# A fused attention and mixer kernel: batch 0's values loaded packed and unpacked by matmuls, a fourth block with a seven-product first layer, whole-half differences, and a new hand-written order

## Chip, cores and metric

One core of a Trainium2 chip runs the whole program. The metric is the device time of one execution in microseconds (us); the figure for a kernel is the median of its runs. The kernel before was measured three times: 341.62, 341.87 and 342.3 us.

## What is computed

The reference, cut to what matters (B=8 batches, H=8 heads, S=576 tokens, Nb=16 beacon rows, D=64):

```python
k_all = concat([beacon_k, k], axis=2); v_all = concat([beacon_v, v], axis=2)
a = softmax(causal(q @ k_all.T / sqrt(D)))          # beacon rows are never masked
x = (a @ v_all), heads side by side                 # 8 x 576 x 512
u = x + (xT @ U @ V).T                              # rank 32, mixes tokens
out = u + relu(u @ w_ch1) @ w_ch2                   # 512 -> 2048 -> 512
```

## The kernel before

**Attention** goes by pairs of heads: 32 pairs, four to a batch. For a pair the queries and keys are regrouped by token (`regroup`, L253), transposed either by PE (`qkT_units`, L261 to L268) or by a DMA transpose whose result is then put in token order by a copy from the tile `raw` (`order_units`, L291), and multiplied in four score visits (L316), each followed by two exponentials on ACT (L321). The causal mask is a minimum on DVE (L304, L306). `av_unit` (L331) multiplies with the values in 15 matmuls of 65 columns; the 65th column of the value tile holds ones, so the row sums come with it, and DVE divides (L339, L340). A batch's result goes through the rank-32 mixing (`mix_units`: qtp L371, ups L390 and L397) into the ring buffer `uT`.

**The mixer** takes `uT` in nine blocks of 512 tokens. Its second layer is always a Strassen-Winograd scheme with seven products P1 to P7 of half size (`product`, L620), for which DVE makes three operand sums per half (`operand_sum`, L601) and closes each product with an addition (`finish`, L645). Its first layer has two forms. Blocks 0 to 5 use sixteen plain units `g` (L529: four matmuls of 512 columns each); blocks 6 to 8 use 28 units `F` (`first_product`, L566: seven products, four pieces each, four matmuls of 256 columns a unit), with weight sums `wf` (L489) and token sums (`token_sum`, L508).

The second layer needs the quarter n3 minus the quarter a11. Before, each `g` unit of the lower half makes that difference on the way out of PSUM: ACT writes the first 256 columns (L533) and DVE the other 256 with a fused relu and subtraction (L534). In the seven-product blocks DVE does it with a fused operation in place (L583), the relu of product 2 is POOL's (L587) and that of product 7 ACT's (L589).

**Loads.** Batch 0's queries and keys come through the queues of SP and ACT (`load_first`); everything else is issued by POOL. `v_loads` (L203) writes values straight into the head-by-head tile `vs`, in five pieces and a beacon load per half or whole batch, so each packet it writes is one head's row of 64 half floats, 128 bytes.

**The order** is written by hand: a string SCRIPT of some 950 steps is walked once, and each step appends its instructions to the engines it uses, which run them in that order. The letters: `Sa` to `Sd` a pair's score visits, `M` the mask, `A` the value products of one head, `G` regroup, `T` transposition or ordering, `R` DMA transpose of a pair, `X` mixing, `g`, `F`, `p`, `P` the mixer's units, `V` a token sum, `U` a transpose of u, `k q v b w` loads, and `I1` one matmul that does no work but keeps PE running (L241). A letter A, V or G inside a step names the engine that copies: ACT, DVE or POOL.

Of the kernel before, what the change touches and what calls it, by code (L numbers as in the profile page):

```python
# [17 lines left out]
P = 128  # L18
# [9 lines left out]
def kernel(  # L28
# [101 lines left out]
    Vsb = const.tile([P, S], F16, name="Vsb", tag="Vsb")  # L130
    ones = const.tile([P, 1], F16, name="ones", tag="ones")
# [66 lines left out]
    def v_loads(src, bsrc, vs, hs):  # L198
        dst = vs[:, :].rearrange("p (c h e) -> p c h e", h=H, e=E)[:, :, hs, 0:D]
        beacon_load(nc.gpsimd, bsrc, dst[:, 0, :, :], hs)  # L200
        for j in range(NT):
            a = Nb if j == 0 else 0
            nc.gpsimd.dma_start(  # L203
                out=dst[a : a + nq[j], j, :, :], in_=src[hs, ds(q0[j], nq[j]), :].rearrange("h p d -> p h d")
            )

# [148 lines left out]
    def mix_units(xb, u0, xt=None, shifted=True):  # L355
# [24 lines left out]
        def part(a, e):  # L380
            n = e - a
            ups = [pst([P, n], F32, name="ups") for _ in range(NCC)]
# [108 lines left out]
    def token_sum(t, i):  # L491
# [16 lines left out]
        nc.vector.tensor_tensor(out=out, in0=a, in1=b, op=ALU.subtract)  # L508

    def block_steps(t, dst):  # L510
# [12 lines left out]
        def g_unit(dc):  # L523
# [8 lines left out]
            if dc < NK:  # L532
                nc.scalar.activation(out=gT[:, dc, 0:H2], in_=g[:, 0:H2], func=AF.Relu)  # L533
                nc.vector.scalar_tensor_tensor(  # L534
                    out=gT[:, dc, H2:512], in0=g[:, H2:512], scalar=0.0, in1=gT[:, dc, 0:H2],
                    op0=ALU.max, op1=ALU.subtract,
                )
            else:
                nc.scalar.activation(out=gT[:, dc, :], in_=g, func=AF.Relu)  # L539
# [4 lines left out]
        def first_product(n, mp):  # L544
# [18 lines left out]
            ps = banks[bank, mp]  # L563
            for i in range(2):
# [14 lines left out]
            else:  # L579
                out, other = {2: (a11, 1), 3: (n3, 6), 7: (a22, 5)}[n]  # L580
                nc.vector.tensor_tensor(out=out, in0=ps, in1=held[other, mp], op=ALU.add)  # L581
                if n == 3:
                    nc.vector.scalar_tensor_tensor(  # L583
                        out=n3, in0=n3, scalar=0.0, in1=a11, op0=ALU.max, op1=ALU.subtract
                    )
                elif n == 2:
                    nc.gpsimd.tensor_scalar_max(out=out, in0=out, scalar1=0.0)  # L587
                else:
                    nc.scalar.activation(out=out, in_=out, func=AF.Relu)  # L589

        def operand_sum(h, j):
# [7 lines left out]
            s2, s1, s4 = (sT[:, i, k, :] for i in range(3))  # L599
            out, x, y, op = ((s2, a22, n3, ALU.add), (s1, s2, a11, ALU.add), (s4, a12, s2, ALU.subtract))[j]  # L600
# [85 lines left out]

    COPY = {"V": nc.vector.tensor_copy, "G": nc.gpsimd.tensor_copy, "A": act_copy}
# [91 lines left out]
    def mix_of(b, part):  # L779
        if b not in mixes:  # L780
            head, parts = mix_units(xbs[b], S * b, xts.get(b))
            mixes[b] = [head] + parts
            for t in range(NBLK - NBR):
                assert 512 * (t + NBR) >= S * (b + 1) or uses[t] == NDC + NCC, (b, t)
# [4 lines left out]
    def step(t):  # L789
# [7 lines left out]
        elif name in "kqbv":  # L797
# [7 lines left out]
            else:  # L805
                v_loads(v[b], beacon_v[b], vss[b % 2], hs)
        elif name == "u":
            late["c"], late["e"], late["s"] = small_loads()
        elif name == "B":
            fill_bigmask()  # L810
        elif name == "s":
# [19 lines left out]
        elif name in "gpUPF":  # L831
# [22 lines left out]
        B I1 GqA0 HqA0 I1 I1 I1 k1A I1 b1 I1 HkV0 GkV0 TkV0 v0A TqA0 Sa0:3 I1 GqG1 u I1 GkV1 TkV1 GkA4  # L854
        I1 Sb0 I1 I1 I1 TqV1 Sd0 q1A Sc0 I1 M0.0 GkV3 I1 I1 Sa1:2 I1 GqV2 I1 Sb1 M0.1 I1 I1 GkG2 I1 TkA2
        TqV2 TkA4 I1 q1B I1 w10 v0B w12 GqA4 I1 Sc1 A0.0 TkV3 Sd1 GqV3 I1 A0.1 Sd2 Sb2 Sa2:1 I1 Sc2 M1.1
        s M1.0 TqV3 GkG5 I1 A1.1 A1.0 Sc3 GqV6 Sa3:1 M2.1 I1 cG I1 I1 GqV5 k1B Sb3 TqV6 I1 Sd3 TqA4 w13
        M2.0 eA k2 M3.1 M3.0 I1 TqA5 A2.1 A2.0 Sc4 Sa4 TkV5 I1 A3.1 GqA7 I1 I1 A3.0 Sd5 Sc5 GkV7 TqV7
        X0.0 Sd4 GkA6 I1 X0.2 X0.1 I1 U0.0 Sa5:0 v1A Sb4 Sb5 g0.8 TkA7 GkV9 M5.1 M4.1 GkV11 M4.0 g0.1
        M5.0 g0.15 g0.0 b2 TkA6 U0.1 GkV8 g0.10 q2 A5.1 A5.0 Sb7 Sa7 Sd7 w11 A4.1 A4.0 g0.11 GqV9 g0.3  # L860
        Sc7 GqV8 M7.1 M7.0 g0.12 Sb6 Sd6 TqV8 TkV9 TkV11 TqV9 g0.2 Sa6:0 GqA11 Sc6 M6.0 v1B g0.14 g0.5
        M6.1 g0.6 g0.9 A6.0 A7.1 A7.0 TkA8 A6.1 w20 g0.13 p00.0 w21 g0.4 Sc9 Sd8 X1.0 g0.7 p01.0 X1.2
        X1.1 p01.1 P01.0 GkV10 p00.1 W0 Sd9 U1.1 TqA11 Sb9 Sa8 W4 W5 W1 P02.0 W2 W3 U0.2 v2 W6 P01.1
        GqA10 Sc8 Sb8 U0.3 M8.1 p00.2 M8.0 P02.1 TkA10 P05.0 Sa9 b3 p01.2 TqA10 P05.1 P06.0 P06.1 A8.0
        b4 k3 GkA13 A8.1 Sa10 Sc10 M9.1 P03.0 P03.1 q3 q4 P07.0 A9.1 g1.9 g1.8 M9.0 A9.0 W7 Sb11 Sc11
        g1.2 g1.7 Sb10 Sd10 M10.0 GqV12 GkV12 R12 g1.1 g1.15 GqA14 Sa11 GqV13 R13 GkA14 R14 Sd11 M11.1
        g1.5 P07.1 g1.3 A10.0 g1.0 TkV12 M11.0 M10.1 g1.6 g1.12 TqA12 GqV16 A11.1 g1.10 TkV13 P04.0 U1.0
        U1.3 TqA13 GkA15 P04.1 g1.14 A11.0 k4 A10.1 Sa13 Sd12 g1.11 p10.0 g1.4 GqA17 g1.13 Sa12 Sb12
        Sc12 p11.0 GqV15 X2.0 M12.0 P11.0 GkA17 P11.1 U1.2 X2.1 GkV16 p11.1 R15 P12.0 P12.1 R16 P16.0
        TqV14 Sd13 Sb13 M12.1 p10.1 p10.2 Sc13 P16.1 b5 U2.2 M13.0 TkA14 v3 A12.1 q5 A12.0 R17 GkA19  # L870
        P15.0 P15.1 p11.2 Sa14 Sd14 Sc14 x12 P17.0 TkV15 M13.1 P13.0 U2.3 A13.0 Sb14 Z16 M14.0 P17.1
# [157 lines left out]
```

## Time and profile before

| what | value |
|---|---|
| median of the runs shown | 341.87 us |
| the profiled execution | 341.91 us |
| its span, first to last instruction | 340.3 us |
| PE, DVE, ACT, POOL busy | 330.1, 263.4, 228.3, 103.6 us |
| first unit of the mixer starts on PE | 36.91 us |
| last matmul starts | near 335 us |

The span is from the first to the last instruction; 1.6 us of the execution lie outside it. PE is the engine that runs the matmuls; its busy time is a union of overlapping spans, so a busy PE says only that some matmul was in flight, and the spacing of matmul starts is the better measure. In the tables a row gives busy time, the mean of one instruction and, after the second bar, how long the engine stood idle before it and for whom. In a timeline row the two first numbers are start and length.

### The profile page before, as it was taken

The numbers are of one execution on the slowest core, as the hardware profiler recorded it, in microseconds if no ns is written. First come the engines' busy times: TensorE is split into PE (matmuls) and PEld (weight loads), VectorE is DVE, ScalarE is ACT, GpSimd is POOL, SyncE is SP. The second block draws the span as 40 slices with busy tenths as digits, with TensorE's granted clock in tenths as the row PEclk, the third lists the DMA queues.
The fourth block names the chain that finished last, engine by engine and source line by source line (L and its number), as shares of the span: only waits on it lengthen the run. The fifth ranks groups of instructions, "written<-read, shape, count | busy, mean of one in ns | idle before, by whom it ended". The sixth has DMA issues, their size and how long they took to land.

```text
span 340.3 us, 8963 instructions
## 1 busy us (share of the span) xinstructions
PE 330.1 (97%) x3527; PEld 227.9 (67%) x3527; DVE 263.4 (77%) x681; ACT 228.3 (67%) x495; POOL 103.6 (30%) x137
## 2 busy tenths in 40 slices
PE   6989999999999999999999999999999999999994
PEld 2456555684668755775577646765688888888883
DVE  3489687994869766984888768885999999896872
ACT  3779987849787889878886798267912842544500
POOL 7787673070530802360015220000001503303300
PEclk9999999999999999999999999999999999999999
DMA  8999999999999998999969998463445501203023
GB/s 170 237 188 167 126 184 197 118 127 213 159 163 189 163 203 127 128 148 191 183 95 145 175 174 115 33 161 99 48 63 159 85 13 63 77 3 94 3 80 128
DMA packets 135600, 44.17 MB, mean 130 GB/s; under 512 B 108384, under 2 KB 130912, under 8 KB 135552
## 3 DMA queue, kind: packets, MB, share of 16 engines
q0 software_dynamic: 69008, 17.54, 60.1%
q1 hardware_dynamic: 65952, 25.66, 39.9%
q8 instruction: 29, 0.48, 0.6%
q10 hardware_dynamic: 592, 0.34, 0.3%
q14 instruction: 19, 0.16, 0.2%
HBM read 37.63 MB, written 9.44 MB: 138 GB/s over the span
## 4 chain that ended last, share of the span: by engine, by line
PE 84%; DVE 10%; issue 2%; ACT 1%; DMA 1%; ACTq 0%; DVEq 0%
PE gps L529 25%; PE cpY L620 17%; PE cpD L620 9%; PE sps L316 8%; PE po L331 8%; PE cpA L620 4%; PE fpY L566 3%; DVE gT L581 3%; PE idle L241 2%; PE tps L263 2%; PE fpD L566 2%; DVE sT L601 1%; DVE ob L645 1%; DMA sth<-in_beacon_k_dram 1%; PE ups L397 1%
## 5 line engine op out<-in xcount | busy, mean ns | idle before, releaser
L321 ACT ACTIVATE expt<-sps 128x496 f16<-128x496 f32 (+2 forms) x256 | 111.6, 543 | 13.4 <-PE sps L316 11.9
L529 PE MATMUL gps<-uT,w 128*128 128x512 f16 x384 | 91.8, 380 | 0.0
L620 PEld LDWEIGHTS <-gT 128*128 128x128 f16 x576 | 54.6, 98 | 10.5 <-issue 2.3
L529 PEld LDWEIGHTS <-w 128*128 128x128 f16 x384 | 34.3, 98 | 37.1 <-issue 2.4
L587 POOL TENSOR_SCALAR gT<-gT 128x512 f16<-128x512 f16 x12 | 17.8, 1493 | 105.7 <-DVE gT L581 89.1
L620 PEld LDWEIGHTS <-sT 128*128 128x128 f16 x432 | 40.8, 98 | 8.0 <-issue 2.0
L203 POOL DMA_DIRECT2D vs<-in_v_dram x50 | 40.8, 838 | 3.8 <-DMA w<-in_moe_w_ch_dram 1.7
L304 DVE TENSOR_TENSOR expt<-expt,bigmask 128x512 f16<-128x512 f16 x64 | 26.9, 421 | 18.8 <-ACT expt L321 18.8
L331 PEld LDWEIGHTS <-expt 128*128 128x128 f16 (+1 forms) x960 | 35.2, 98 | 8.7 <-DVE expt L304 1.1
L539 ACT ACTIVATE gT<-gps 128x512 f16<-128x512 f32 x48 | 29.3, 618 | 15.4 <-PE gps L529 14.9
L331 PE MATMUL po<-vs,expt 128*128 128x65 f16 (+1 forms) x960 | 37.8, 194 | 0.7 <-DVE expt L304 0.6
L620 PE MATMUL cpY<-wsum,gT 128*128 128x256 f16 x288 | 36.1, 273 | 0.0
L620 PE MATMUL cpD<-w,sT 128*128 128x256 f16 x288 | 35.6, 273 | 0.3 <-DVE sT L601 0.3
L316 PE MATMUL sps<-qT,kT 64*128 64x80 f16 (+4 forms) x384 | 34.3, 284 | 0.2 <-DVE qT L265 0.2
L340 DVE TENSOR_TENSOR xb<-po,rec 128x320 f16<-128x320 f32 x64 | 31.5, 492 | 2.2
L534 DVE SCALAR_TENSOR_TENSOR gT<-gps,gT 128x256 f16<-128x256 f32 x48 | 19.7, 420 | 13.0 <-ACT gT L533 12.9
L109 ACT ACTIVATE hP<-fpY 128x512 f32<-128x512 f32 x24 | 13.7, 597 | 23.1 <-PE fpY L566 22.0
L533 ACT ACTIVATE gT<-gps 128x256 f16<-128x256 f32 x48 | 18.9, 412 | 12.2 <-PE gps L529 11.9
L316 PEld LDWEIGHTS <-kT 64*128 64x128 f16 x384 | 13.8, 94 | 19.8 <-issue 11.1
L645 DVE TENSOR_TENSOR ob<-cpY,ut 128x512 f32<-128x512 f32 (+1 forms) x28 | 18.7, 667 | 5.9 <-PE cpY L620 5.9
L566 PEld LDWEIGHTS <-wf 128*128 128x128 f16 x192 | 18.6, 98 | 3.1 <-issue 0.7
L620 PE MATMUL cpY<-w,gT 128*128 128x256 f16 x144 | 17.7, 273 | 0.0
(118 smaller groups left out, 484.7 us busy)
## 6 DMA issues: line engine op xcount, KB each, us to landing
out_dram<-ob SPq DMA_DIRECT2D x16, 512.0 KB, 4.7
st<-in_k_dram POOLq DMA_DIRECT2D x6, 512.0 KB, 8.0
st<-in_q_dram POOLq DMA_DIRECT2D x6, 512.0 KB, 8.3
vs<-in_v_dram POOLq DMA_DIRECT2D x18, 128.0 KB, 7.9
w<-in_moe_w_ch_dram POOLq DMA_DIRECT2D x4, 512.0 KB, 7.5
w<-in_moe_w_ch_dram POOLq DMA_DIRECT2D x2, 1024.0 KB, 12.0
stm<-in_k_dram SPq DMA_DIRECT2D x4, 256.0 KB, 6.0
out_dram<-ob SPq DMA_DIRECT2D x4, 256.0 KB, 2.8
```

The costliest lines, as they stand in the source:

```text
L203: nc.gpsimd.dma_start(out=dst[a : a + nq[j], j, :, :], in_=src[hs, ds(q0[j], nq[j]), :].rearrange("h p d -> p h d"))
L304: nc.vector.tensor_tensor(out=e4, in0=e4, in1=bigmask, op=ALU.min)
L316: nc.tensor.matmul(ps[i][:, ds(o, w)], kT[hp, c, ds(P * ch, P)], qT[hp, c, ds(qa, w)], start=True, stop=True,)
L321: nc.scalar.activation(out=ex[i][:, ds(PAD + SLOT * g, gw[g])], in_=ps[i][:, 0 : gw[g]], func=AF.Exp, scale=scale)
L331: nc.tensor.matmul(po[:, j, :], ex[0 : nk[c], ds(blk[(c, j)], P)], vs[0 : nk[c], ds(c * H * E + h * E, E)], start=(c == 0), stop=(c == j),)
L340: nc.vector.tensor_tensor(out=xb[:, h // 2, :, ds(D * (h % 2), D)], in0=po[:, :, 0:D], in1=r.broadcast_to([P, NT, D]), op=ALU.mult)
L529: nc.tensor.matmul(g, w1[:, cc, ts(dc, P)], uT[:, cc, ds(ring(t0), 512)], start=(cc == 0), stop=(cc == NCC - 1))
L534: nc.vector.scalar_tensor_tensor(out=gT[:, dc, H2:512], in0=g[:, H2:512], scalar=0.0, in1=gT[:, dc, 0:H2], op0=ALU.max, op1=ALU.subtract,)
L539: nc.scalar.activation(out=gT[:, dc, :], in_=g, func=AF.Relu)
L566: nc.tensor.matmul(ps[:, i, :], a[:, kk, ts(2 * mp + i, P)], b[:, kk, :], start=opens and i == 0 and kk == 0, stop=kk == 1, skip_group_che ...
L620: nc.tensor.matmul(ps[:, i, :], a[:, f, ds(P * i, P)], b[:, f, :], start=opens and i == 0 and f == 0, stop=f == NK - 1, skip_group_check=True,
L645: nc.vector.tensor_tensor(out=out, in0=ps[:, ii, :], in1=other, op=ALU.add)
```

## The change

1. **Batch 0's values.** `packed_loads` brings 448 of the 576 tokens in one load, four tokens to a partition, on 112 partitions (`vf`), so that each packet holds four tokens of one head. The first 112 tokens, the last 16 and the beacon rows still go straight to `vs`. Four `unpack` steps then put the packed tokens in place: four matmuls of 512 columns against a selection matrix `pick`, and one copy from PSUM. `fill_pick` makes that matrix with a memset and four copies on DVE.
2. **Block 5's first layer** becomes 28 `F` units instead of 16 `g` units, with four token sums of its own. Blocks 5 to 8 now have that form.
3. **Bulk differences.** n3 minus a11 is made once per half, by one DVE subtraction of 128x1024 ahead of the first operand sum, in all nine blocks. The `g` units all leave PSUM by one ACT relu of 512 columns; the fused DVE operations L534 and L583 are gone. The relu of products 2, 3 and 7 runs on the engine that the step names: 21 on POOL, 20 on DVE, 7 on ACT.
4. **The order** is new from end to end. 24 `I1` steps stand in it instead of 37. Of the 40 ordering copies from `raw`, POOL takes 24 (before none), DVE 7 and ACT 9 (before 20 each); POOL also takes 22 more of the regrouping copies.

```diff
+    def packed_loads(src, bsrc, vs, vf):
+        dst = vs[:, :].rearrange("p (c h e) -> p c h e", h=H, e=E)[:, 0, :, 0:D]
+        nc.gpsimd.dma_start(
+            out=vf[0:VP], in_=src[:, nq[0] : nq[0] + VP * VJ, :].rearrange("h (p j) d -> p h (j d)", j=VJ)
+        )
+        nc.gpsimd.dma_start(out=dst[Nb : Nb + nq[0]], in_=src[:, 0 : nq[0], :].rearrange("h p d -> p h d"))
...
+    def unpack(vf, vs, c, copy):
+        ps = pst([P, H, D], F32, name="vps")
+        n = min(P, VP * VJ - P * (c - 1))
+        rows = ds(VG * (c - 1), n // VJ)
+        for j in range(VJ):
+            nc.tensor.matmul(
+                ps[0:n], pick[rows, ds(VJ - 1 - j, n)], vf[rows, :, ds(D * j, D)], start=(j == 0), stop=(j == VJ - 1)
+            )
+        copy(out=vs[0:n, :].rearrange("p (c h e) -> p c h e", h=H, e=E)[:, c, :, 0:D], in_=ps[0:n])
...
-            if dc < NK:
-                nc.scalar.activation(out=gT[:, dc, 0:H2], in_=g[:, 0:H2], func=AF.Relu)
-                nc.vector.scalar_tensor_tensor(
-                    out=gT[:, dc, H2:512], in0=g[:, H2:512], scalar=0.0, in1=gT[:, dc, 0:H2],
-                    op0=ALU.max, op1=ALU.subtract,
-                )
-            else:
-                nc.scalar.activation(out=gT[:, dc, :], in_=g, func=AF.Relu)
+            nc.scalar.activation(out=gT[:, dc, :], in_=g, func=AF.Relu)
...
-                if n == 3:
-                    nc.vector.scalar_tensor_tensor(
-                        out=n3, in0=n3, scalar=0.0, in1=a11, op0=ALU.max, op1=ALU.subtract
-                    )
-                elif n == 2:
-                    nc.gpsimd.tensor_scalar_max(out=out, in0=out, scalar1=0.0)
-                else:
-                    nc.scalar.activation(out=out, in_=out, func=AF.Relu)
+                RELU[eng](out)
...
+            if j == 0:
+                nc.vector.tensor_tensor(out=n3, in0=n3, in1=a11, op=ALU.subtract)
...
-        B I1 GqA0 HqA0 I1 I1 I1 k1A I1 b1 I1 HkV0 GkV0 TkV0 v0A TqA0 Sa0:3 I1 GqG1 u I1 GkV1 TkV1 GkA4
+        HkA0 I1 I1 B I1 I1 GkV0 b1 I1 GqG0 f0 I1 HqV0 TqV0 TkA0 Sa0:3 Sb0 GkV1 TkV1 Sd0 I1 q1A GqG1 TqV1
```

Three places of the new order, as each engine gets it. First POOL's queue just after the start. `st` and `hd` are the staging tiles of batch 1's queries and keys, `vs` batch 0's values, `stm` the loaded queries and keys of batch 0. Before:

```order
L716 MEMSET vs_127 128x40
L196 DMA st_191<-in_k_dram 128x4x256
L190 DMA hd_189<-in_k_dram 64x4x64
L193 DMA hd_189<-in_beacon_k_dram 16x8x64
L193 DMA vs_126<-in_beacon_v_dram 16x4x64
L203 DMA vs_126<-in_v_dram 112x4x64
L203 DMA vs_126<-in_v_dram 128x4x64 x3
L203 DMA vs_126<-in_v_dram 80x4x64
L253 CAST pr<-stm 128x512
```

After:

```order
L748 MEMSET vs_128 128x40
L205 DMA hd_195<-in_beacon_k_dram 16x8x64
L287 CAST pr<-stm 128x512
L221 DMA vf<-in_v_dram 112x8x256
L224 DMA vs_127<-in_v_dram 112x8x64
L226 DMA vs_127<-in_v_dram 16x8x64
L205 DMA vs_127<-in_beacon_v_dram 16x8x64
L208 DMA st_198<-in_q_dram 128x4x256
```

Batch 1's keys no longer stand ahead of the values; a regrouping copy, which waits for batch 0's first queries, now does. Four loads carry the whole of batch 0's values; before, six carry half of them and six more follow later.

Second, PE in the first pairs, after the second pair's score visit `Sc1` (`sps` are score tiles, `tps` transposed heads, `idle` the matmuls without work). Before, at the visits ahead of the third pair's transposes:

```order
L316 MATMUL sps_326<-qT,kT_124 128x464
L316 LDWEIGHTS kT_124
L316 MATMUL sps_327<-qT,kT_124 128x464
L241 LDWEIGHTS ident
L241 MATMUL idle<-ident 128x512
...
L261 LDWEIGHTS hd_141
L261 MATMUL tps<-ident,hd_141 128x80
```

After:

```order
L236 MATMUL vps<-vf,pick 128x512
L350 LDWEIGHTS kT_125
L350 MATMUL sps_332<-qT,kT_125 128x208
...
L350 MATMUL sps_339<-qT,kT_125 128x464
L275 LDWEIGHTS ident
L275 MATMUL idle<-ident 128x512
...
L236 MATMUL vps<-vf,pick 64x512
L295 LDWEIGHTS hd_142
L295 MATMUL tps<-ident,hd_142 128x80
```

One unpacking group of four matmuls now stands ahead of the visits `Sd1` and `Sb1`, and three more groups ahead of the third pair's transposes; the `...` behind the idle matmul stand for two more of those and eleven unpacking matmuls.

Third, DVE where block 5's first layer ends. Before it takes half of each lower `g` unit:

```order
L534 SCALAR_TENSOR_TENSOR gT<-gps,gT 128x256
L291 COPY qT<-raw 128x512
L534 SCALAR_TENSOR_TENSOR gT<-gps,gT 128x256
L339 RECIPROCAL rec<-po 128x5
L340 TENSOR_TENSOR xb<-po,rec 128x5x64
```

After, it joins the pieces of the products 2, 3 and 7 and takes some of their relus (`TENSOR_SCALAR`):

```order
L613 TENSOR_TENSOR gT<-fpA,hP_4538 128x2x256
L441 TENSOR_TENSOR uT<-ups,xt 128x336 x4
L545 TENSOR_TENSOR tb<-uT,tb 128x512
L613 TENSOR_TENSOR gT<-fpA,hP_4594 128x2x256
L613 TENSOR_TENSOR gT<-fpY,hP_4545 128x2x256
L715 TENSOR_SCALAR gT<-gT 128x2x256
```

The ordering copy from `raw` is gone from DVE here, and the mixing of batch 6 (`uT<-ups,xt`) stands between the pieces.

More of the change, by code (lines that the diff above doesn't have):

```diff
@@ L806, in step @@
                 v_loads(v[b], beacon_v[b], vss[b % 2], hs)
+        elif name == "f":
+            late["f"] = stage.tile([P, H, 4 * D], F16, name="vf", tag="st0")
+            packed_loads(v[0], beacon_v[0], vss[0], late["f"])
+        elif name == "D":
+            unpack(late["f"], vss[0], int(arg[1:]), COPY[arg[0]])
         elif name == "u":
@@ L810, in step @@
             fill_bigmask()
+            fill_pick()
         elif name == "s":
```

140 lines of the change are left out of this document (83 added, 57 removed).

## The prediction

> **What bounds the kernel now.** First the page, for the span and the busy times.
>
> ```profile
> span 340.3 us, 8963 instructions
> ...
> PE 330.1 (97%) x3527; PEld 227.9 (67%) x3527; DVE 263.4 (77%) x681; ACT 228.3 (67%) x495; POOL 103.6 (30%) x137
> ```
>
> PE is busy 97% of the span, but busy spans of matmuls overlap. So I ask next what PE waited for after its first mixer unit, which the chain of waits puts at 36.91 us (its row stands below), and then what all engines did in that stretch: in its row PE, PEld, DVE, ACT and POOL follow the length.
>
> ```profile
> PE fpD L566 <- DVE ob L645: 0.5, 1, 0.5
> PE cpD L620 <- DVE sT L601: 0.3, 1, 0.3
> ```
>
> ```profile
> 36.90:335.30 298.40, 297.45 (x3174) 210.89 (x3172) 238.89 (x586) 201.06 (x429) 75.85 (x87) 1.00 0.98 122
> ```
>
> Two waits, 0.8 us in all, over 298.4 us: from 36.9 us on the kernel is one queue of matmuls, and the others keep up (DVE 239 us, ACT 201, POOL 76). There a change is worth what it takes from or adds to PE's own work. Before 36.9 us it is otherwise:
>
> ```profile
> 27.00:36.90 9.90, 9.84 (x169) 6.47 (x167) 8.33 (x28) 9.89 (x28) 5.18 (x8) 1.00 1.50 160
> ```
>
> ```profile
> L241 PE MATMUL idle<-ident 128*128 128x512 f16 x36 | 13.1, 453 | 1.7 <-POOL ident masks.py:199 1.6
> ```
>
> ```profile
> ACT expt L321 <- PE sps L316: 4.4, 6, 1.6
> ```
>
> PE looks full there too, but over the start 13.1 us of it are the 36 matmuls without work. ACT is the pacemaker: 9.89 of the last 9.9 us, and its waits for scores in the whole start come to 4.4 us, six of them. So a change in the start pays only if ACT, or what feeds it, gets through sooner.
>
> **The change, part by part.** The working is made for the profiled execution of 341.91 us (340.3 of span and 1.6 outside it), 0.04 above the median of the runs shown, so it carries over as it is.
>
> *Block 5's first layer.* The chain of waits has stretches of matmuls without a gap:
>
> ```profile
> 36.91 0.97 PE gps L529 x4
> 38.15 2.59 PE gps L529 x12
> ...
> 41.87 0.91 PE po L331 x30
> ...
> 294.13 1.75 PE fpY L566 x16
> ```
>
> A matmul of 512 columns takes 2.59/12 = 0.216 us, one of 256 columns 1.75/16 = 0.109. The sixteen `g` units are 64 x 0.216 = 13.8 us, the 28 `F` units 112 x 0.109 = 12.25. **-1.56 us**, in a stretch where PE waits for nothing. What the edit puts on DVE is priced together with the next one:
>
> ```profile
> L534 DVE SCALAR_TENSOR_TENSOR gT<-gps,gT 128x256 f16<-128x256 f32 x48 | 19.7, 420 | 13.0 <-ACT gT L533 12.9
> ...
> L601 DVE TENSOR_TENSOR sT<-gT 128x1024 f16<-128x1024 f16 x18 | 12.3, 688 | 3.1 <-ACT gT L539 2.7
> ...
> L581 DVE TENSOR_TENSOR gT<-fpY,hP 128x512 f16<-128x512 f32 x12 | 8.0, 684 | 0.5 <-ACT hP L109 0.4
> ...
> L291 DVE COPY kT<-raw 128x512 f16<-128x512 f16 x10 | 6.1, 606 | 0.8 <-DMA raw<-pr 0.8
> ```
>
> *Bulk differences and DVE's load.* Block 5 costs DVE twelve joinings, 12 x 0.684 = 8.2 us, and four token sums, at most 0.688 each, 2.8. The fused operation goes from all 48 lower `g` units, 48 x 0.420 = 20.2, and from twelve pieces of blocks 6 to 8, which I price like a joining, 8.2. Eighteen bulk subtractions have the shape of `sT`: 18 x 0.688 = 12.4. Of the 20 relus on DVE the trace has no row; by elements they lie between half of `sT`, 0.34, and a whole one, 0.69, and I take 0.5: 10. Thirteen ordering copies leave: 13 x 0.606 = 7.9. The balance is 8.2 + 2.8 + 12.4 + 10 - 20.2 - 8.2 - 7.9 = -3, between -6 and +1: DVE's load stays. It is worth nothing in PE's time, being hidden behind PE's queue as long as DVE has some 59 of 298 us free; without that cover each 0.69 us subtraction stands directly in front of P6, then P5. ACT's eight half-wide evacuations a block become full ones, but it has 97 us free there and gives up eleven ordering copies.
>
> *Copies moved to POOL.* POOL takes on 24 ordering copies, 22 regroupings and 9 more relus.
>
> ```profile
> L321 ACT ACTIVATE expt<-sps 128x496 f16<-128x496 f32 (+2 forms) x256 | 111.6, 543 | 13.4 <-PE sps L316 11.9
> ...
> L587 POOL TENSOR_SCALAR gT<-gT 128x512 f16<-128x512 f16 x12 | 17.8, 1493 | 105.7 <-DVE gT L581 89.1
> ```
>
> ```profile
> L109 ACT ACTIVATE pr<-st 128x512 f16<-128x512 f16 x23 | 14.8, 652 | 4.3 <-DMA st<-in_k_dram 4.3
> ...
> L109 ACT ACTIVATE kT<-raw 128x512 f16<-128x512 f16 x10 | 11.1, 1116 | 0.0
> ```
>
> ```profile
> 21.55 0.64 POOL L253 COPY pr<-st 128x512 f16<-128x512 f16 x1
> ```
>
> POOL's one regrouping copy took 0.64. Its ordering copy has no row: at least 0.64, at most the relu's 1.49. On ACT ordering takes 1.116/0.652 = 1.7 times a regrouping, which gives 1.1 on POOL, and that I take. POOL then does 22 x 0.64 + 24 x 1.1 + 9 x 1.49 = 54 us more, some 158 of 340, hidden behind PE's queue of matmuls. Behind each copy on POOL stand the loads of later batches, and a load that waits until its tile is free holds the copies behind it; those are waited for by the scores.
>
> The Trainium skill speaks against this part ("SBUF — State Buffer", Who interferes with whom): a DVE instruction with two SBUF inputs and a POOL instruction that reads SBUF use one port under an exclusive lock, and the later one waits the other out. The trace hardly bears it out: the mean of POOL's twelve relus is 1.49 us beside a busy DVE, with no bare one to compare. By the rule the sum stays as it is unless POOL's queue runs late.
>
> *The keep-warm matmul behind the start.* One `I1` of the mixed part goes: **-0.22**.
>
> *The start.* Up to the first mixer unit the new order does more: the two heads of pair 4, 30 `po` matmuls or 0.91 us, and two more transposed pairs less one score visit, about 0.3 (four transposes are 0.39 in the rows below, an estimate for the difference). **-1.2**, if the first unit starts at the same time. Whether it does:
>
> - PE gets 16 unpacking matmuls, 16 x 0.216 = 3.45 us, and loses 12 without work, 2.59: +0.86.
> - ACT, up to the first cast of `u`, makes three copies fewer for q and k and two more for the values, 0.65 each, and one score visit more, 2 x 0.543: +0.4.
> - Against that, POOL issues batch 0's values in four loads, not twelve. In the stretch where it wrote the second half of them, DVE's cast of a small head tile took 1.16 us, and the reciprocal behind it had to wait:
>
> ```profile
> 10.13 0.63 PE L263 MATMUL tps<-ident,pr 128*128 128x128 f16 x4
> ...
> 12.56 0.39 PE L263 MATMUL tps<-ident,pr 128*128 128x128 f16 x4
> ...
> 20.53 1.16 DVE L741 CAST hd<-sth 80x128 f16<-80x128 f32 x1
> ```
>
> If it falls to the size of a regrouping, 0.64 or less, 0.5 or more comes back. The three make about **0** for the first unit's time, between gains and costs of under 1 us. Bounds: the whole unpacking on the path, +3.45; three quarters of ACT's 4.4 us of waits gone, -3.3.
>
> Sum: -1.56 - 0.22 - 1.2 + 0 = -3.0 us; 341.9 - 3.0 = **338.9**.
>
> **The rivals.**
>
> *The start gets shorter still* (0.13). For it: batch 1's keys no longer stand ahead of the values, and most of batch 0's values come in packets of four tokens. Against it: ACT has as much to do as before. With 3.3 us of its waits gone, 335.6.
>
> *The unpacking comes late, and the kernel is slower* (0.14). PE runs in order; the first unpacking group stands ahead of `Sd1` and `Sb1`, and ACT's next exponentials come from these.
>
> ```profile
> st<-in_q_dram POOLq DMA_DIRECT2D x6, 512.0 KB, 8.3
> ...
> w<-in_moe_w_ch_dram POOLq DMA_DIRECT2D x2, 1024.0 KB, 12.0
> ```
>
> ```profile
> 4.97 0.63 ACT L109 ACTIVATE pr<-stm 128x512 f16<-128x512 f32 x1 [1.05 <-DMA stm<-in_q_dram]
> ```
>
> The packed load (448 KB by its shape) can be issued once batch 0's first queries have landed and POOL has regrouped them, near 5.6 us, where ACT's regrouping of the same data ends now. At 8.3 us to landing it is there at 14, about when PE arrives. At 12 it is 3.7 late, and so is the second pair's rest: 342.6. It eats the whole gain from a landing near 17 us on.
>
> *POOL's copies come late* (0.10). The 11 taken from ACT end later by 1.49 - 1.12 and the 13 from DVE by 1.49 - 0.61 at the dear end, 15.5 us together; if a fifth of that gets through the order's slack to PE, 342.0.
>
> *The first layer gains nothing* (0.08). The new products want twelve joinings from DVE within some 12 us of PE's time, beside the attention's masks; if DVE sets the pace, PE waits as much as it saves: 340.5.
>
> *PE stays at half speed longer* (0.05). The same four transposes took 0.63 us at 10.13 and 0.39 at 12.56, though the granted clock reads 1.00 throughout. Fewer matmuls without work could move that step behind the unpacking, whose 16 matmuls would then take twice 0.216 each: +3.45, 342.3. The Trainium skill ("TensorE: Matmul & The Clock Gate", Part 1: The HAM clock gate) has it as a rule that the clock is halved until a window of sustained matmul activity has passed. The rows agree with the rule; that the removed matmuls decide the moment, none shows.
>
> **How the numbers follow.** The forecast has 0.50: the order behind the start leaves PE so little to wait for that its work is the time. The range leaves out the far side of the slower rival and reaches down to the shortest start: 335.6 to 342.3. Faster by over 0.2% (0.7 us, about what a measurement of this kernel can tell from no change): the forecast, the shorter start and the fourth rival, 0.71, and 0.03 of the late copies, 0.74. Within 0.2%: 0.12, the rest of the late copies and the half speed. Slower: 0.14.
>
> **What would show it.** Right: a first mixer unit near 37 us with pair 4's first two heads done before it; block 5's 256-column matmuls still 0.109 apart; hardly a wait of PE behind that. Wrong: PE waiting for `vf`; ACT idle between 14 and 25 us; PE waiting for `kT` or `qT` from POOL; waits on `sT` or on the joined pieces in block 5; ordering copies on POOL beyond 1.5 us. The forecast as a whole fails if PE's waits behind the first mixer unit exceed some 3 us.

## The result, and the profile after

The changed kernel takes 351.10 us (median of four runs, 350.86 to 352.56); the kernel before, run beside it, 341.75 us (341.40 to 342.30). The ratio is 1.0281, 95% interval 1.0249 to 1.0312: slower by 9.4 us, where 3.0 us faster was forecast. Ratios here leave out disturbed runs while medians hold every run, which is why the two disagree for the quarter copies below.

The page of the profiled execution (351.01 us):

```profile
span 349.3 us, 9102 instructions
...
PE 331.9 (95%) x3578; PEld 232.6 (67%) x3578; DVE 271.6 (78%) x658; ACT 219.0 (63%) x467; POOL 153.7 (44%) x187
...
PE 60%; DVE 29%; issue 4%; DMA 3%; ACT 2%; SPq 0%; DVEq 0%; ACTq 0%
```

PE is still busy 95% of the span, so the busy shares say little. DVE did not lose 3 us but gained 8.2 (263.4 to 271.6). PE's waits name DVE:

```profile
PE po L365 <- DVE expt L338: 2.3, 4, 0.9
PE cpD L647 <- DVE sT L628: 1.9, 2, 1.3
...
PE fpY L598 <- DVE gT L613: 1.1, 2, 0.6
PE sps L350 <- DVE xb L374: 0.7, 3, 0.3
PE cpY L647 <- DVE sT L628: 0.5, 1, 0.5
PE po L365 <- DVE expt L340: 0.5, 1, 0.5
PE sps L350 <- DVE uT L441: 0.5, 2, 0.3
PE cpD L647 <- DVE ob L672: 0.4, 1, 0.4
PE gps L567 <- ACT gT L570: 0.2, 1, 0.2
```

Nearly every wait behind the start is for DVE, and none for a `kT` or `qT` from POOL. The first mixer unit, in PE's timeline:

```profile
36.95 1.09 PE L365 MATMUL po<-vs,expt 128*128 128x65 f16 x30
37.87 0.38 PE L275 MATMUL idle<-ident 128*128 128x512 f16 x1
38.09 1.02 PE L567 MATMUL gps<-uT,w 128*128 128x512 f16 x4
```

It starts at 38.09 us, 1.2 later than before (36.85 by the matmul's own start there), with pair 4's two heads ahead of it as forecast.

To see where the 9.0 us of span went I add up PE's order of matmuls, charging each its undisturbed spacing (0.216 us for 512 columns, 0.109 for 256, others on the straight line through these two), and call the rest between starts a gap. Some matmuls run side by side, so work and gaps together exceed the elapsed time; the differences are what counts.

| behind the first mixer unit | before | after | difference |
|---|---|---|---|
| it starts at, us | 36.85 | 38.09 | +1.2 |
| PE's work | 310.80 | 307.77 | -3.0 |
| gaps | 17.5 | 27.7 | +10.2 |
| of these over 0.16 us | 1.9 (6) | 12.7 (27) | +10.8 |

PE's work fell by the 3.0 us of the forecast. Gaps of 10.2 us came in its place (0.6 us of the 9.0 is left over by matmuls side by side). So the question is why PE now waits 27 times, mostly for DVE. The DVE groups of the changed kernel that answer to the `expt` and `sT` rows of before:

```profile
L338 DVE TENSOR_TENSOR expt<-expt,bigmask 128x512 f16<-128x512 f16 x64 | 30.7, 479 | 16.7 <-ACT expt L355 16.5
L374 DVE TENSOR_TENSOR xb<-po,rec 128x320 f16<-128x320 f32 x64 | 31.5, 492 | 2.2
L340 DVE TENSOR_TENSOR expt<-expt,mask 80x80 f16<-80x80 f16 x64 | 16.4, 256 | 0.0
L628 DVE TENSOR_TENSOR sT<-gT 128x1024 f16<-128x1024 f16 x18 | 13.6, 755 | 2.7 <-ACT gT L570 1.6
L526 DVE TENSOR_TENSOR wf<-w 128x1024 f16<-128x1024 f16 x4 | 3.6, 895 | 0.0
```

And the same two masks of the kernel before:

```profile
L304 DVE TENSOR_TENSOR expt<-expt,bigmask 128x512 f16<-128x512 f16 x64 | 26.9, 421 | 18.8 <-ACT expt L321 18.8
L306 DVE TENSOR_TENSOR expt<-expt,mask 80x80 f16<-80x80 f16 x64 | 12.1, 190 | 0.0
```

The same instruction on the same shape grew from 421 to 479 ns, and from 190 to 256; `sT` from 688 to 755, `wf` from 682 to 895. `xb`, whose large input is in PSUM, kept its 492, also the seven that ran beside an ordering copy (491 to 493). Taken one by one, the masks L338 that overlap no POOL instruction last 418 ns (median), the seven that overlap most with an ordering copy 868 in the mean. One of them, first DVE's timeline, then POOL's, over the same 3 us:

```profile
150.46 0.68 DVE L672 TENSOR_TENSOR ob<-cpY,ut 128x512 f32<-128x512 f32 x1
151.06 2.25 DVE L338 TENSOR_TENSOR expt<-expt,bigmask 128x512 f16<-128x512 f16 x1
153.24 0.18 DVE L340 TENSOR_TENSOR expt<-expt,mask 80x80 f16<-80x80 f16 x1
```

```profile
150.95 1.07 POOL L325 COPY kT<-raw 128x512 f16<-128x512 f16 x1
151.96 1.06 POOL L325 COPY qT<-raw 128x512 f16<-128x512 f16 x1
```

This mask starts behind a POOL copy and lasts until the second one is through: 2.25 us for 0.42 us of work. PE's next value products wait for it.

### The profile page after: what moved, and what is told of

The parts are those of the page before. It is cut to its first block, busy times and chain, and to the rows that moved or that the text cites. A ratio compares the mean times of both kernels' runs of the same rounds, so it can differ in the third digit from the quotient of the medians.

```text
span 349.3 us, 9102 instructions
## 1 busy us (share of the span) xinstructions
PE 331.9 (95%) x3578; PEld 232.6 (67%) x3578; DVE 271.6 (78%) x658; ACT 219.0 (63%) x467; POOL 153.7 (44%) x187
## 4 chain that ended last, share of the span: by engine, by line
PE 60%; DVE 29%; issue 4%; DMA 3%; ACT 2%; SPq 0%; DVEq 0%; ACTq 0%
PE gps L567 14%; PE cpY L647 12%; PE cpD L647 8%; PE sps L350 6%; PE po L365 5%; DVE gT L613 5%; DVE sT L628 4%; PE fpY L598 3%; DVE xb L374 3%; DVE uT L441 2%; DVE ob L672 2%; DVE expt L338 2%; PE fpD L598 2%; DMA raw<-pr 2%; DVE gT L626 2%
## 5 line engine op out<-in xcount | busy, mean ns | idle before, releaser
L355 ACT ACTIVATE expt<-sps 128x496 f16<-128x496 f32 (+2 forms) x256 | 112.0, 552 | 26.1 <-PE sps L350 19.9
L567 PE MATMUL gps<-uT,w 128*128 128x512 f16 x320 | 76.5, 380 | 0.4 <-ACT gT L570 0.2
L716 POOL TENSOR_SCALAR gT<-gT 128x512 f16<-128x512 f16 x21 | 31.3, 1507 | 80.8 <-DVE gT L613 66.6
L647 PEld LDWEIGHTS <-gT 128*128 128x128 f16 x576 | 54.3, 98 | 10.4 <-issue 2.3
L570 ACT ACTIVATE gT<-gps 128x512 f16<-128x512 f32 x80 | 47.5, 637 | 19.0 <-PE gps L567 18.4
L567 PEld LDWEIGHTS <-w 128*128 128x128 f16 x320 | 29.0, 98 | 33.3 <-issue 3.9
L647 PEld LDWEIGHTS <-sT 128*128 128x128 f16 x432 | 40.9, 98 | 10.8 <-DVE sT L628 3.4
L338 DVE TENSOR_TENSOR expt<-expt,bigmask 128x512 f16<-128x512 f16 x64 | 30.7, 479 | 16.7 <-ACT expt L355 16.5
L109 ACT ACTIVATE hP<-fpY 128x512 f32<-128x512 f32 x32 | 18.7, 599 | 33.8 <-PE fpY L598 25.4
L350 PE MATMUL sps<-qT,kT 64*128 64x80 f16 (+4 forms) x384 | 36.7, 285 | 1.3 <-DVE xb L374 0.7
L647 PE MATMUL cpD<-w,sT 128*128 128x256 f16 x288 | 35.3, 273 | 2.3 <-DVE sT L628 1.9
L647 PE MATMUL cpY<-wsum,gT 128*128 128x256 f16 x288 | 36.8, 273 | 0.0
L287 POOL COPY pr<-st 128x512 f16<-128x512 f16 x23 | 16.1, 712 | 43.6 <-DMA raw<-pr 16.6
L215 POOL DMA_DIRECT2D vs<-in_v_dram x40 | 33.0, 844 | 0.7 <-DMA st<-in_k_dram 0.6
L350 PEld LDWEIGHTS <-kT 64*128 64x128 f16 x384 | 14.1, 94 | 22.8 <-issue 14.6
L598 PEld LDWEIGHTS <-wf 128*128 128x128 f16 x256 | 24.7, 98 | 3.3 <-issue 0.3
L325 POOL COPY kT<-raw 128x512 f16<-128x512 f16 x12 | 13.5, 1130 | 25.9 <-DMA raw<-pr 25.9
L598 PEld LDWEIGHTS <-w 128*128 128x128 f16 x192 | 18.7, 98 | 3.9 <-issue 1.7
```

The costliest lines, as they stand in the source:

```text
L215: nc.gpsimd.dma_start(out=dst[a : a + nq[j], j, :, :], in_=src[hs, ds(q0[j], nq[j]), :].rearrange("h p d -> p h d"))
L338: nc.vector.tensor_tensor(out=e4, in0=e4, in1=bigmask, op=ALU.min)
L350: nc.tensor.matmul(ps[i][:, ds(o, w)], kT[hp, c, ds(P * ch, P)], qT[hp, c, ds(qa, w)], start=True, stop=True,)
L355: nc.scalar.activation(out=ex[i][:, ds(PAD + SLOT * g, gw[g])], in_=ps[i][:, 0 : gw[g]], func=AF.Exp, scale=scale)
L567: nc.tensor.matmul(g, w1[:, cc, ts(dc, P)], uT[:, cc, ds(ring(t0), 512)], start=(cc == 0), stop=(cc == NCC - 1))
L598: nc.tensor.matmul(ps[:, i, :], a[:, kk, ts(2 * mp + i, P)], b[:, kk, :], start=opens and i == 0 and kk == 0, stop=kk == 1, skip_group_che ...
```

## The experiments

Theories: **the port** (POOL's copies read SBUF and lock out DVE's instructions with two SBUF inputs, which then make PE wait); **lateness** (POOL's copies end later, and the scores wait); **bulk differences or block 5** (they stand on DVE in front of PE); **the order** itself. Times are medians, with the ratio to the kernel before, run on the same chip.

| run | us | ratio, 95% |
|---|---|---|
| the changed kernel | 351.10 | 1.0281 (1.0249 to 1.0312) |
| ordering copies back | 356.35 | 1.0443 (1.0423 to 1.0463) |
| all moved copies back | 370.38 | 1.0854 (1.0830 to 1.0877) |
| before, with spare copies | 355.21 | 1.0410 (1.0381 to 1.0438) |
| before, with spare memsets | 367.35 | 1.0775 (1.0740 to 1.0809) |
| copies write-only | 343.28 | 1.0048 (1.0020 to 1.0075) |
| copies and relus write-only | 347.09 | 1.0163 (1.0123 to 1.0203) |
| before, bulk differences alone | 347.81 | 1.0195 (1.0163 to 1.0226) |
| before, packed values alone | 352.12 | 1.0333 (1.0266 to 1.0401) |
| ordering on ACT | 355.92 | 1.0438 (1.0404 to 1.0473) |
| block 5 plain | 351.77 | 1.0323 (1.0281 to 1.0365) |
| quarter copies | 351.37 and 351.11 | 1.0178 and 1.0182 (1.012 to 1.024) |
| write-only, fused differences | 348.05 | 1.0202 (1.0157 to 1.0248) |
| before, packed values gated | 354.08 | 1.0348 (1.0316 to 1.0380) |
| relus on ACT | 356.68 | 1.0455 (1.0438 to 1.0472) |
| write-only, relus on ACT | 347.21 | 1.0178 (1.0159 to 1.0196) |

### Copies taken back from POOL

```diff
-        ... TkG12 A10.0 P04.1 q4 TqG13 ...
+        ... TkV12 A10.0 P04.1 q4 TqA13 ...
```

> The changed kernel, with the 24 ordering copies that it gave to POOL back on the engine that made them before the change (about half DVE, half ACT), at the same places of the order. Port theory (POOL's copies lock the SBUF port that DVE's two-input instructions need): the masks L338 fall from 479 ns to near 430, the sums sT from 726 to near 690, and two thirds of the 10 us that PE lost behind the start come back, although DVE takes 12 more copies: 343 to 346 us. Lateness theory (POOL's copies simply end later, and the scores wait): the copies end in time again, so the same 343 to 346. Rival, bulk differences and block 5 on DVE: no gain, DVE is fuller by 7 us: 350 to 354. Rival, the new order itself: 350 to 352.

356.35 us: slower, against the port theory's 343 to 346. Set against the changed kernel matmul by matmul (PE's order is the same), PE gains at four places 0.97, 0.77, 0.66 and 1.45 us. The last three were waits for a mask or `sT` that had been stretched; the mask's mean fell to 430 ns. At the first, the mask itself had not been stretched, but it stood behind a regrouping copy of DVE that took 1.01 us beside a POOL copy; where POOL does nothing beside it, such a copy takes 0.28. In the changed kernel, DVE's timeline, then POOL's:

```profile
87.52 1.01 DVE L287 COPY pr<-st 128x512 f16<-128x512 f16 x1
88.45 0.41 DVE L338 TENSOR_TENSOR expt<-expt,bigmask 128x512 f16<-128x512 f16 x1
```

```profile
87.32 1.06 POOL L325 COPY kT<-raw 128x512 f16<-128x512 f16 x1
```

That DVE copy has only one input, so POOL's copies hold up more than the two-input instructions of the theory. But the run loses more than these gains, in new waits:

```profile
PE cpY L647 <- DVE ob L672: 2.5, 2, 2.3
PE sps L350 <- DVE kT L325: 1.8, 1, 1.8
...
PE sps L350 <- ACT qT L109: 1.2, 1, 1.2
```

```profile
L325 DVE COPY kT<-raw 128x512 f16<-128x512 f16 x9 | 5.8, 639 | 4.0 <-DMA raw<-pr 4.0
```

The row of DVE's ordering copies says why: DVE reached them before the transposed data had landed and stood idle 4.0 us (0.8 in the kernel before). The new order puts these copies where POOL may wait for a DMA; DVE and ACT run in order, and all behind the copy waits too. So the run does not speak against the port, but cannot price it. The second edit treats 19 regrouping copies alike:

```diff
-        GkV15 TkG13 Sd13 GqV15 R15 Sc13 g1.11 TqV12 g1.12 p11.0 Sa13 Sd12 TqG14 Sb13 GqG16
+        GkV15 TkV13 Sd13 GqV15 R15 Sc13 g1.11 TqV12 g1.12 p11.0 Sa13 Sd12 TqV14 Sb13 GqV16
```

> As the run before, and 19 regrouping copies taken back from POOL as well. Port theory: POOL reads SBUF hardly more than before the change, so DVE's durations are those of before (masks near 420 ns) and nearly all of the 10 us comes back: 340 to 343 us. Lateness theory: regroupings stand early in the order, with time to spare, so it stays near the run before, within 1 us. Bulk differences or the order as the cause: 350 to 354.

370.38 us. DVE's masks are back at 418 ns, as the port theory has it, and the kernel is 19 us slower still, for the reason just given:

```profile
L287 DVE COPY pr<-st 128x512 f16<-128x512 f16 x33 | 10.1, 314 | 15.6 <-DMA raw<-pr 9.3 <-DMA st<-in_q_dram 4.6 <-DMA st<-in_k_dram 1.7
```

### The kernel before, with a busier POOL

```diff
+            for m in range(2):
+                if arg[0] == "T":
+                    src = raw_of[p][:, i, :, 64 * m : 64 * m + 64].rearrange("x j p -> x p j")
...
+                nc.gpsimd.tensor_copy(out=dst, in_=src)
```

> The kernel before, in which POOL makes 43 spare copies beside its own work, right behind those ordering and regrouping copies that the change moves to POOL: each reads the same data (in two halves) into a tile that nobody reads. The work on DVE, ACT and PE is that of before, and nothing waits for a spare copy but POOL itself. Port theory: DVE's masks L304 grow from 421 ns to over 450 and the sums sT from 688 to over 710, and the kernel becomes slower by 3 to 10 us: 345 to 352. Lateness theory, bulk differences, the order: none of them is in this kernel, so 341.5 to 343 (POOL's loads a little later).

> The kernel before with POOL as long busy at the same places, but with memsets, which write SBUF and read nothing (and a copy of one element ahead of them, which keeps the place). Port theory: DVE's two-input instructions keep their time (masks near 421 ns), and the kernel stays within 1 us of before, 341 to 343. If POOL's occupation itself, or its writes, are the cost, it comes out like the run with spare copies, 345 or more.

The masks behave as the port theory says. With spare copies, then with memsets:

```profile
L305 DVE TENSOR_TENSOR expt<-expt,bigmask 128x512 f16<-128x512 f16 x64 | 29.4, 459 | 18.3 <-ACT expt L322 18.3
```

```profile
L305 DVE TENSOR_TENSOR expt<-expt,bigmask 128x512 f16<-128x512 f16 x64 | 26.8, 418 | 19.0 <-ACT expt L322 19.0
```

The times do not: 355.21 with copies, 367.35 with memsets, and in both PE waits for something else, here with copies, then memsets:

```profile
PE po L332 <- DMA vs<-in_v_dram: 9.7, 5, 4.3
```

```profile
PE po L332 <- DMA vs<-in_v_dram: 17.7, 9, 7.9
```

The spare work waits on POOL for its transposed data, and behind it in POOL's queue stand the loads of the values. Both expectations on the time fall: the spares measure late loads. PE's waits for the stretched masks came to only 0.4 us; in the order before, DVE had slack where they fell.

### The deciding run: the same places, no reads

```diff
+    def write_only(out, in_):
...
+        nc.gpsimd.tensor_copy(out=gate2, in_=in_[0:1, 0:1])
+        for _ in range(2 if len(out.shape) == 3 else 1):
+            nc.gpsimd.memset(out, 0.0)
```

> The changed kernel; the 43 ordering and regrouping copies that the change moved to POOL stand where they stood, on POOL, and wait for what they waited for, but each is a copy of one element and one or two memsets of the target, about as long as the copy and with no input to read (left out: the queries and keys of these pairs are zero). Port theory: nothing of POOL locks DVE's inputs any more, the masks L338 fall to near 420 ns, the sums sT to near 690, and PE gets back most of the 10 us lost behind the start: 340 to 344 us. Lateness theory: the copies' targets are ready no earlier than before, so 349 to 352. Bulk differences, block 5's products, or the order as the cause: 349 to 352.

343.28 us: 7.8 of the 9.4 us are back. POOL was as busy (153.8 us) and at the same places. Counted in PE's progress, 37 of its 43 targets were ready no earlier, the other six by at most 1.5 us. In the profile the mask is back at

```profile
L338 DVE TENSOR_TENSOR expt<-expt,bigmask 128x512 f16<-128x512 f16 x64 | 26.7, 418 | 17.5 <-ACT expt L355 17.3
```

and of the large waits of the changed kernel there remain

```profile
PE fpY L598 <- DVE gT L613: 1.0, 2, 0.6
PE po L365 <- DVE expt L338: 0.8, 3, 0.3
PE cpD L647 <- DVE sT L628: 0.6, 1, 0.6
PE cpY L647 <- DVE sT L628: 0.5, 1, 0.5
```

PE's gaps behind the first mixer unit are 21.1 us (27.7 with the copies), DVE's busy time 260.2 us (271.6). Set beside the changed kernel, PE gains 0.55, 0.77, 1.45 and 0.66 us at the same four places as in the first run. So it is the reads of POOL's copies, as the port theory has it, and not their lateness, since next to nothing came earlier. That these pairs' data are zero here does not explain it either: beside the spare memsets, with all data in place, the masks took 418 ns too. The first place gains less (0.55 for 0.97) because DVE's regrouping copy there still took 0.57 us beside the memsets (0.28 in the first run, which got all 0.97 back): for that copy, writes count as well.

```diff
-        "G": lambda t: nc.gpsimd.tensor_scalar_max(out=t, in0=t, scalar1=0.0),
+        "G": lambda t: relu_write_only(t),
...
+        for _ in range(3):
+            nc.gpsimd.memset(t, 0.0)
```

> As the run before, with POOL's 21 relus made write-only in the same way (left out: these quarters of the first layer's result are zero). Port theory: the last stretches of DVE, three or four instructions in the blocks 5 to 8, go too: 0.3 to 1.5 us faster than the run before. If the relus' lateness is what PE waits for in these blocks, no difference to the run before, within 0.3 us.

347.09 us: slower, not faster. The write-only relu takes 3 x 0.53 + 0.19 = 1.8 us against 1.5, and the operand sums now wait for it (`PE cpY L647 <- DVE sT L628` 2.0 us, DVE before that for POOL's `gT` 1.8). A faulty test of the port, but it shows how little room POOL's relus have.

### The other parts of the change

```diff
-                nc.scalar.activation(out=gT[:, dc, 0:H2], in_=g[:, 0:H2], func=AF.Relu)
...
+            if j == 0:
+                nc.vector.tensor_tensor(out=n3, in0=n3, in1=a11, op=ALU.subtract)
```

> The kernel before, its order and its engines unchanged, with the bulk differences alone: the lower g units leave through ACT whole, the relu of product 3 is DVE's, and one subtraction of 128x1024 stands ahead of the first operand sum of each half. The prediction's term for it is nothing, 341 to 342.5. Theory that bulk differences put DVE in PE's way: each of the 18 subtractions stands for up to 0.69 us in front of P6 and P5, 345 to 354, with waits of PE for sT. Port theory: no POOL copy is added, so 341 to 343.

347.81 us, though DVE is busy 253.5 us, 10 less than before. The waits:

```profile
PE cpD L613 <- DVE sT L594: 1.6, 2, 1.0
PE cpY L613 <- DVE ob L638: 1.4, 2, 1.2
PE cpY L613 <- DVE sT L594: 1.2, 1, 1.2
```

Work that DVE did in small pieces under the first layer now comes in one piece in front of the sums that P6 and P5 need. That is 4.7 us of new gaps in an order not made for it. The reverse, in the changed order and without the lock (blocks 0 to 4):

```diff
-            nc.scalar.activation(out=gT[:, dc, :], in_=g, func=AF.Relu)
+            if dc < NK:
+                nc.scalar.activation(out=gT[:, dc, 0:H2], in_=g[:, 0:H2], func=AF.Relu)
+                nc.vector.scalar_tensor_tensor(
...
-            if j == 0:
+            if j == 0 and t >= 5:
```

> The run with POOL's moved copies write-only (343.3 us), with the bulk differences of blocks 0 to 4 undone: their lower g units leave half by ACT and half by DVE's fused relu and subtraction again (left out, as there: queries and keys of the pairs concerned are zero). If the bulk differences are what keeps that run above the forecast (each stands on DVE in front of P6), 341 to 342.5. If DVE's load counts (40 fused operations of 0.42 for ten of 0.69, 10 us more on DVE), 344 to 348.

348.05 us: there the bulk form is worth some 5 us, so in blocks 0 to 4 it is not what keeps the write-only run above the forecast; in blocks 5 to 8 it was not tried. With the fused form DVE is busy 269.0 instead of 260.2 us, and PE waits for its masks:

```profile
PE po L365 <- DVE expt L338: 2.6, 5, 1.3
```

Block 5, with sixteen `g5` steps in the places of the 28 `F5` steps:

```diff
-        ... M31.0 F51.0 F55.0 F52.0G X6.2 U6.2 V5.3 F55.2 F56.0 F51.2 F51.1
+        ... M31.0 g5.13 X6.2 U6.2 g5.11 g5.4 g5.2
```

> The changed kernel with block 5's first layer in its former form: sixteen units g in the places of the 28 units F, no token sums of block 5. PE does 1.56 us more. By the prediction's term the time grows by it, 352 to 353.5. If DVE's joinings and relus set the pace in block 5, the plain form gives PE back its waits there (a cpY and a fpY of 0.7 us each, and part of an sT): 349.5 to 351.

351.77 us. PE's work is 1.59 us more, as the prediction's term had it; the time's interval overlaps that of the changed kernel, so whether the whole 1.6 arrives stays undecided.

Batch 0's packed values in the order before (`f0` where `k1A` was, four `D` steps ahead of the second and third pairs), then with the first regrouping of queries on POOL ahead of the load:

```diff
-        B I1 GqA0 HqA0 I1 I1 I1 k1A I1 b1 I1 HkV0 GkV0 TkV0 v0A TqA0
+        B I1 GqA0 HqA0 I1 I1 I1 f0 I1 b1 I1 HkV0 GkV0 TkV0 k1A TqA0
```

> The kernel before, with batch 0's values loaded packed and unpacked by 16 matmuls and four copies, and nothing else changed (all 37 matmuls without work stay). The prediction's term for the start, without the fewer idle matmuls: 0 to +2 us, 341.5 to 344. If the packed load is what shortens a start, 338 to 341. If PE comes to wait for vf, 345 or more.

```diff
-        B I1 GqA0 HqA0 I1 I1 I1 f0 I1 b1
+        B I1 GqG0 HqA0 I1 I1 I1 f0 I1 b1
```

> The kernel before with the packed values as in the run of packed values alone, but with the first regrouping of queries on POOL and the packed load behind it, as in the changed kernel's queue. If that run lost its 10 us because the packed load went out ahead of batch 0's queries and keys and took their bandwidth, it now starts like the changed kernel, with the first mixer unit near 38 to 40 us: 341.5 to 345. If unpacking is what PE waits for in that order, the first mixer unit stays beyond 44 us: 349 or more.

352.12 and 354.08 us; the first mixer unit starts at 47.0 and 49.4 us, and behind it the gaps are those of before (17.2, 17.1). Both numbers lie where a wait for the unpacking was to put them, but that is not the reason: PE waits 5.0 and 7.4 us for ACT's exponentials, and not for `vf`. ACT's timeline of the first of the two runs has most of the cause:

```profile
9.37 1.06 ACT L355 ACTIVATE expt<-sps 128x496 f16<-128x496 f32 x2 [1.09 <-PE sps L350]
17.08 0.63 ACT L109 ACTIVATE pr<-st 128x512 f16<-128x512 f16 x1 [6.65 <-DMA st<-in_k_dram]
17.62 2.40 ACT L355 ACTIVATE expt<-sps 128x464 f16<-128x464 f32 x6
```

In the order before, ACT regroups batch 1's keys (`GkA4`) early, and I had put their load behind the values. ACT waits 6.65 us for it, the exponentials with it; gated, 8.69 us (the first mixer unit is 10.1 and 12.5 us late; the rest is not traced). The changed kernel has that regrouping later and on POOL. So these two runs price my edit, not the packed load, which was not tried by itself in an order that suits it.

### Other places for the copies and relus

```diff
-        ... TkG12 A10.0 P04.1 q4 TqG13 ...
+        ... TkA12 A10.0 P04.1 q4 TqA13 ...
```

> The changed kernel with its 24 ordering copies of POOL on ACT, at the same places. ACT has over 100 us idle, and its copies took 1.12 us, about what POOL's take. Port theory: with these copies gone from POOL, DVE's masks and sums fall back as in the first run, and no copy is added to DVE: 344 to 348 us if ACT has the time where the copies stand. If ACT's exponentials then come late behind copies that wait for their transposed data, 352 to 358, as the first run had it with half of them on ACT.

355.92 us: slower. PE gets the port's share back at the same places (0.97, 0.77, 1.45 and 0.66 us) and loses more where ACT is late: `PE sps L350 <- ACT expt L355` 2.9 us, the longest 2.6, behind copies for which ACT stood idle 4.1 us waiting for data.

```diff
+    def in_quarters(out, in_):
+        for m in range(4):
+            nc.gpsimd.tensor_copy(out=out[:, ds(32 * m, 32)], in_=in_[:, ds(32 * m, 32)])
```

> The changed kernel with each of POOL's 24 ordering copies made as four copies of 128x128. Port theory, if the lock is held for one instruction: DVE gets in between the quarters, the longest mask falls from 2.25 us to under 1, and PE gets back some of the 8 us: 345 to 349. If DVE waits until POOL's whole run of copies is through, nothing is won, or POOL's longer total costs: 350 to 353.

> The quarter copies once more, in more rounds, since the first measurement ran from 346 to 358 us. If DVE waits for one instruction and not for POOL's whole run, undisturbed runs lie at 346 to 349, below the changed kernel's 351; if only the first measurement's spread made it look faster, 350 to 353.

The ten runs lie between 345.5 and 358.1 us. The four that the ratios count (346.0, 349.0, 345.5, 349.7) are below the changed kernel, the medians are not. The two profiles are of the longest runs; in both, the longest mask L338 is 0.82 us instead of 2.25, so DVE does get in between quarters. Whether the split pays is not settled; POOL's 96 quarters take 45.9 us where 24 copies took 29.0.

```diff
-        ... F51.0 F55.0 F52.0G ... F52.1G F57.0V F55.3 F56.2 F53.2G
+        ... F51.0 F55.0 F52.0A ... F52.1A F57.0A F55.3 F56.2 F53.2A
```

> The changed kernel with all relus of products 2, 3 and 7 on ACT: 21 come from POOL (1.5 us each), 20 from DVE (0.3 us each). ACT has most of its time free in blocks 5 to 8. If these relus are late, or hold up DVE, PE's waits for sT and for the joined pieces there shrink: 347.5 to 350.5. Port theory, since POOL's copies stay: no more than that. If ACT's relus stand behind its copies hP: 351 to 354.

> The run with POOL's moved copies write-only, and the relus of products 2, 3 and 7 all on ACT (left out, as there: queries and keys of the pairs concerned are zero). PE's work is 3.0 us less than before the change; what kept the write-only run from the forecast are 3.6 us more of gaps and the start. If most of these gaps are the late relus, 339.5 to 341.5; if they are the joinings and subtractions themselves, 342.5 to 344.

356.68 and 347.21 us: both slower than their counterparts. The waits for joined pieces and `sT` at the ends of blocks 5 and 6 do shrink (0.75, 0.70 and 0.75 us gained), but ACT's relus stand in front of its copies of the held products:

```profile
PE fpY L598 <- ACT hP L109: 4.1, 7, 1.0
```

Moved to ACT as a whole, the relus cost more than they give back. No run gave a kernel faster than the one before.

## Why the prediction was wrong

**The step that failed** is "Copies moved to POOL" with its "hidden behind PE's queue of matmuls", and in it the sentence "The trace hardly bears it out". The rule was set aside because the mean of POOL's own relus showed nothing. What could show it is the row of a DVE instruction beside a relu. Most of these show nothing either: in the kernel before, DVE's fused operation with both inputs in SBUF runs wholly inside a relu and takes the 0.69 us of its twelve; DVE's timeline, then POOL's:

```profile
268.85 0.69 DVE L583 SCALAR_TENSOR_TENSOR gT<-gT 128x512 f16<-128x512 f16 x1
```

```profile
268.23 1.48 POOL L587 TENSOR_SCALAR gT<-gT 128x512 f16<-128x512 f16 x1 [1.27 <-DVE gT L581]
```

But one in that same trace does: a token sum took 0.84 us, where others of its length take 0.42. Again DVE's timeline, then POOL's:

```profile
263.95 0.84 DVE L508 TENSOR_TENSOR tb<-uT 128x512 f16<-128x512 f16 x1
```

```profile
263.79 1.59 POOL L587 TENSOR_SCALAR gT<-gT 128x512 f16<-128x512 f16 x1 [0.36 <-DVE gT L581]
```

So the failure was twofold: the sign was overlooked, and a relu, which holds DVE up for a part of its length only (see the last section), was let stand for a copy. POOL's copies do hold DVE up (418 to 868 ns), and the trace of before had next to no copy beside a mask. For copies the rule of the Trainium skill ("SBUF — State Buffer", Who interferes with whom) is borne out: two SBUF inputs wait (the masks), one input from PSUM does not (`xb`, 492 ns), and a POOL instruction that only writes does not contend with them (masks of 418 ns beside memsets). Its claim that the later one waits out the whole instruction does not hold for POOL's relus above.

**"DVE's load stays"** was right without the lock: forecast -3 us, the write-only run has 260.2 against 263.4, -3.2. That the two agree so closely is luck: DVE's 20 relus came to 6.6 us there, not 10, and copies that the sum left out made up for it. With the lock it is +8.2.

**"It is worth nothing in PE's time"** was wrong, and without this the lock would have cost little. 11.4 us on DVE (271.6 against 260.2) went with 7.8 us of time, 8.8 us (the fused differences) with some 5. DVE has 59 us free on average, but not in front of the waits: one stretched instruction in a busy stretch delays all that follow on DVE, and PE with them. For 20 of the 27 large gaps of the changed kernel, DVE's unbroken stretch of work ahead of the gap holds over 0.3 us of added duration, three of them through POOL's relus.

**PE's work**: -1.56, -0.22 and -1.2 were forecast, -3.0 in sum; measured -3.03.

**The start** was forecast at no later first unit. It came 1.2 us later here, and between 0.4 and 1.9 later in the profiles of nine other runs with the same start. The term's -1.2 was thus about used up; which of its three parts was mis-sized no run separates. `vf` was issued at 6.0 us, landed 7.0 later, and PE did not wait for it: the rival of the late unpacking did not occur.

**POOL's copies come late** was the right list of instructions with the wrong mechanism. They took 1.13 and 1.30 us in the mean (forecast 1.1; four of the 24 passed the 1.5 that was named as a sign of being wrong), POOL's busy time grew by 50.1 us (forecast 54), and no matmul waited for them. The test that the prediction set itself, waits of PE beyond 3 us behind the first mixer unit, is what decided: 7.9 us (0.8 of the rows above fall ahead of that unit, and three rows of 0.2 are not shown there).

**What stays open**: 1.6 us between the write-only run and the kernel before, where the forecast had -3.0. The start has 1.1 of the 4.6; PE's gaps, 3.6 us more than before, sit largely in blocks 5 to 8, at joined pieces and `sT`. Moving the relus to ACT showed that these waits can be had back, but only for others of the same size. POOL's relus still read SBUF in the write-only run, and six DVE instructions in blocks 5 to 8 are longer beside them there, by 2.0 us in all; whether this, the relus' lateness or the joinings themselves make these gaps, no run separates.

## What to carry to other kernels

Before moving copies to POOL, list what DVE runs beside them: those with both inputs in SBUF can wait, so could DVE's regrouping copies with one input there, and those with one input in PSUM did not. The quiet row of another POOL operation proves nothing for a copy. An engine that is 80% busy hides little: ask where its unbroken stretches end in a wait of PE, and count every us added there at half or more (7.8 of 11.4 here). A copy that waits for a DMA belongs on an engine whose queue can stand still, so taking it back without moving its place tests the place, not the engine.

## What the hardware showed that was not expected

A copy and a relu on POOL, which both read SBUF, hold DVE up for different stretches. Take a held instruction's undisturbed length off its end, and it ran from about 0.13 us before the copy's end; beside a relu it ran from 1.01 to 1.02 us before the end, some 0.47 us into a relu of 1.48, in all seven cases with two inputs in the traces of before and after (one DVE relu, with one input, was held to near the end, 0.67 us for 0.29). A two-input instruction that started between 0.1 and 0.43 us into a relu was held (a token sum of 0.84 us for 0.42, in the changed kernel a `sT` of 0.91 for 0.69, a small mask of 0.60 for 0.19); the fused operation shown above started 0.62 us into its relu, and was not. Why a relu lets go so early, no run shows. Nor is DVE's wait bounded by one POOL instruction: with two copies back to back the mask took 2.25 us for 0.42 of work. It works both ways: POOL's ordering copy, 1.05 us at its shortest, took up to 2.56. And POOL's queue passes waits on: spare work that waited there for data held back the values' loads until PE had waited 17.7 us for them.
